# Scores and masked part of y in 64x64 tiles, without the quarter of later tokens, and with another order of the steps within a pair

## The chip, the cores and the metric

The kernel runs on one core of a Trainium2 chip. Its time is the device time of one execution in microseconds (us). The engines are named as in the profile: PE is TensorE (PEld its weight loads, PEq, SPq and so on the queues in front of the engines), DVE is VectorE, ACT is ScalarE, POOL is GpSimd, SP starts the DMA transfers. All data are float32.

## The reference

Gated linear attention over 32 independent heads (4 batches, 8 heads, 768 tokens, width 48), and behind it a soft mixture of 8 experts with 4 slots each over the 384 columns of all heads of a batch:

```python
f = 1.0 / (1.0 + np.exp(-f_logit))
for t in range(S):
    state = f[:, :, t, :, None] * state + np.einsum('bhd,bhe->bhde', k[:, :, t], v[:, :, t])
    y[:, :, t] = np.einsum('bhd,bhde->bhe', q[:, :, t], state)
...
logits = x @ phi
...
slot_input = d.T @ x          # d: softmax of the logits over all tokens
...
    h = np.maximum(slot_input[e] @ w1[e], 0.0)
    slot_out[e] = h @ w2[e]
...
return (c @ slot_out)         # c: softmax of the logits over the slots
```

## The kernel before

**Pairs and chunks.** Two heads make a pair (i, 16 of them, 4 to a batch), and stand on partitions 0 to 47 and 64 to 111. The 768 tokens are six chunks of 128 (m). Within a chunk the gates become running sums `L` of log f, and k is multiplied by exp(L), q by exp(-L). Then y of a chunk is the sum of two products: the masked one, v times the scores k q with the later keys set to 0 (steps `sc`, `mask`, `ia`), and the one with the state at the chunk's start (`kt`, `kv`, `scan`, `ie`).

**The steps of a pair,** by their names in the code, in the profile and in the listing below:

- ACT: `e`, `ln` (L324, L328, tile fb): the gates. `g`, `p` (L335, L338, tiles gb, pb): exp(L) and exp(-L). `ye`, `xe` (yT, xb): copies out of PSUM.
- DVE: `L` (L332, tile Lb): the running sum over 768 elements, from two SBUF inputs. `mask` (L378, scb from sc): two of them to a pair, 768 elements a partition each, from PSUM. `scan` (L411, sb): the state over the chunks. `kte` (L315, kta): copy out of PSUM.
- POOL: `dk`, `dq` (L341, tiles kb, qb): the products of k with exp(L) and q with exp(-L). `pbx` (L315), `pend` (L353): copies of the chunks' ends. Once per batch `cdiv` (L539, ce) and `j4` (L516, pin).
- PE: `kt` (L361): k turned; `sc` (L373): scores; `kv` (L407); `ia` (L398, y from scb and va): the masked product; `ie` (L421, y from qb and sb); `lg` (L453, pl): logits; `xtr` (L432, xt): y turned. Per batch also `te`, `tl` (L471 to L473), `pi` (L496), `ct` (L545).

The array of PE can be used as one, as two halves by rows or by columns, or in quarters of 64x64. Each step names its mode: `sc` "rows" (two tiles of 64x128), `kv` and `ia` "cols" (two of 128x64), `ie` "quarters", `lg` "strips" (four of 128x32), the others "square". A float32 matrix product is two records in the trace: 12 products of `sc` are 24.

**What sets the order.** Each step is an `op` with a due time (`z = i * T`, T = 7.0). For every engine the steps are sorted by due time before anything else is decided, and the engine works them off in that order. Where a step waits, all behind it on its engine wait too. SP's transfers are placed by a planner with costs; the weight loads (`lw1`, `lw2`) are paced behind the steps of that plan and go to buffers of the attention once these are free. PSUM has three units of 1024 columns (a) and two of 512 (b), and three buffers each of k and q and two each of L, g, p and the scores lie between the pairs.

**After the last pair** come the slots' inputs, the two expert layers (`up` L619, `down` L665) and the output (`comb` L711), from about 119 us on.

Of the kernel before, what the change touches and what calls it, by code (L numbers as in the profile page):

```python
# [11 lines left out]
ALU = mybir.AluOpType  # L12
AX = mybir.AxisListType

B, H, S, D = 4, 8, 768, 48
C = 128
# [7 lines left out]
PW = 112  # L24
# [186 lines left out]
def gla_soft_moe_kernel(ctx: ExitStack, tc: tile.TileContext, q, k, f, v, vt, phi, w1, w2, out):  # L211
# [35 lines left out]
    scb = [P([128, 2, 2, 3, C], f"scb{i}") for i in range(N_SC)]  # L247
# [22 lines left out]
    mask = P([128, C], "mask")  # L270
# [15 lines left out]
    nc.gpsimd.affine_select(mask, mask, pattern=[[1, C]], compare_op=ALU.is_ge, fill=0.0, base=0, channel_multiplier=-1)  # L286
# [56 lines left out]
    def decay_k(o, i, cs):  # L343
        times(o, kb[i % N_K][:PW, cs], gb[i % N_G][:PW, cs])
# [21 lines left out]
    def score(o, i, h):  # L366

        u = unit(("sc", i, h))
        for m in range(3):
            cs = slice(C * (3 * h + m), C * (3 * h + m) + C)  # L370
            for r in range(2):
                rs = slice(64 * r, 64 * r + D)
                nc.tensor.matmul(  # L373
                    u[:, 512 * r + C * m : 512 * r + C * m + C], kb[i % N_K][rs, cs], qb[i % N_Q][rs, cs], start=True, stop=True,
                )

    def score_mask(o, i, h):
        nc.vector.tensor_tensor(  # L378
            scb[i % N_SC][:, :, h], un["sc", i, h].rearrange("p (r x) -> p r x", r=2)[:, :, : 3 * C].rearrange("p r (m t) -> p r m t", t=C),
            mask.unsqueeze(1).unsqueeze(1).broadcast_to([128, 2, 3, C]), op=ALU.mult,  # L380
        )
# [9 lines left out]
    def intra(o, i, h):  # L391
        u = unit(("y", i)) if h == 0 else un["y", i]
        for m in range(3 * h, 3 * h + 3):
            for r in range(2):
                at = 1 - r if m < SWAP else r

                v0 = 576 * (i % N_V) + 96 * m + D * r
                nc.tensor.matmul(  # L398
                    u[rows(at), y_cols(m)], va[:, v0 : v0 + (D if at else 64)], scb[i % N_SC][:, r, h, m % 3],
                    start=m % 3 == 0, stop=False, skip_group_check=True,  # L400
                )
# [326 lines left out]
    def warm(due, n, us=0.9):  # L728
# [3 lines left out]
    warm(-100, 4, 1.6)  # L732
# [6 lines left out]
        e=(-99, -98), ln=(-97, -96), g=(-94, -91), p=(-93, -90),  # L739
# [3 lines left out]
    for n, (name, i) in enumerate(  # L743

        [("e", 1), ("ln", 1), ("e", 2), ("kte", 0), ("pbx", 0), ("g", 1), ("p", 1), ("ln", 2), ("ye", 0), ("g", 2), ("p", 2)]

        + [("L", 1), ("scan", 0), ("dq", 1), ("L", 2)]

        + [("dk", 1), ("pend", 0)]
    ):  # L750
        START[name, i] = -80 + n
    START["e", 1], START["ln", 1], START["L", 1] = -95, -92, -94
# [4 lines left out]
    def attention(i):  # L757
# [35 lines left out]
        usual = dict(e=-2 * T - 6.9, ln=-2 * T - 5.9, L=-2 * T + 2.2, g=-2 * T + 4.4, dk=-2 * T + 3.8, p=-2 * T + 4.8, dq=-2 * T + 5.6)  # L793
# [5 lines left out]
        op("pbx", {"POOL": 0.65} if i else {"ACT": 0.4}, decay_pbx, i, r=PB, w=[PX], due=START.get(("pbx", i), z - T + 0.7))  # L799
        op("pend", {"POOL": 0.2}, decay_pend, i, r=PB, w=[("pends", i)], due=START.get(("pend", i), z - T + 1.3))  # L800
        if i == 0:
            for h in range(2):
                op(("kt", "square"), {"PE": 0.33}, kt, i, 3 * h, 3 * h + 3, r=K[h : h + 1], x=[KT], w=[KK], due=START["kt"][h], take=[] if h else [(KK, "a")], ni=6)
        else:
            op(("kt", "square"), {"PE": 0.65}, kt, i, r=K, x=[KT], w=[KK], due=z - T + 3.9, take=[(KK, "a")], ni=12)
        op("kte", {"DVE": 0.86} if i else {"ACT": 0.86}, kt_copy, i, r=[KK], w=[KT], due=START.get(("kte", i), z - T + 4.6), free=[KK])
        for h, key in enumerate((S0, S1)):
            op(("sc", "rows"), {"PE": 0.7}, score, i, h, r=[K[h], Q[h]], x=[SC[h]], w=[key], due=START["sc"][h] if i == 0 else z - T + 5.3 + 0.7 * h, take=[(key, "a")], ni=24)
            op("mask", {"DVE": 0.95}, score_mask, i, h, r=[key], w=[SC[h]], due=START["mask"][h] if i == 0 else z - T + 6.1 + h, free=[key])
        if i == 0:  # L810
            warm(-94, 1)
        op(("kv", "cols"), {"PE": 0.71}, kv, i, r=[KT, V], x=[SB], w=[KV], due=z, take=[(KV, "b")], ni=48)
        op("scan", {"DVE": 0.76}, state, i, r=[KV, PX], w=[SB], due=START.get(("scan", i), z + 1.2), free=[KV])
        for h in range(2):
            op(("ia", "cols"), {"PE": 0.66}, intra, i, h, r=[SC[h], V, *([YY] if h else [])], x=[] if h else [Y], w=[YY], due=z + 0.7 + 0.66 * h, take=[] if h else [(YY, "a")], ni=24)
        op(("ie", "quarters"), {"PE": 0.72}, inter, i, r=[*Q, SB, YY], w=[YY], due=z + 2.2, ni=40)
        op("ye", {"ACT": 0.82}, y_copy, i, r=[YY], w=[Y], due=START.get(("ye", i), z + 3.3), free=[YY])
# [311 lines left out]
```

## Time and profile before

| | us |
|---|---|
| three runs | 174.04, 175.64, 175.8 |
| median of them | 175.64 |
| the profiled execution | 174.06 |
| its span in the profile | 171.9 |
| attention, from the first scores (8.75) to the last pair's (114.3) | 105.5 |
| PE busy, DVE, ACT, POOL | 155.5, 115.8, 93.8, 88.9 |

The span goes from the first to the last instruction; 2.2 us of the profiled execution lie outside it. Of a group of instructions the page gives busy time and the mean of one; the chain gives what was waited for last, from the end back to the start; the timeline gives start and duration.

### The profile page before, as it was taken

Reading aid. Unit: us, or ns where it says so; the run is one execution under the profiler, and the core shown is the slowest. Engines: PE = TensorE matmul, PEld = TensorE weight load, DVE = VectorE, ACT = ScalarE, POOL = GpSimd, SP = SyncE. Lnnn points to the kernel's source line nnn. Section 1 sums busy time; section 2 is a strip of 40 time slices with the busy share of each in tenths; the row PEclk is TensorE's granted clock in tenths of the full one; section 3 lists DMA queues with packets and bytes.
Section 4 is the critical chain, followed back from the end, with each engine's and each line's share of the span. In section 5 each row is a group of like instructions: output and inputs, shape, how many; then the busy total and the mean of one; then the engine's idle time right before and its main releaser. Section 6 shows DMA issues by size and latency. Waiting matters only on the chain.

```text
span 171.9 us, 6033 instructions
## 1 busy us (share of the span) xinstructions
PE 155.5 (90%) x2548; PEld 121.3 (71%) x2548; DVE 115.8 (67%) x168; ACT 93.8 (55%) x168; POOL 88.9 (52%) x88
## 2 busy tenths in 40 slices
PE   5959999999899998999998999999899999989810
PEld 2347888988788968889886889888555454568600
DVE  2677999889998995898996989756540333144420
ACT  5892897867677758678683783542421211042410
POOL 3074599888499895897996988841000001000000
PEclk9999999999999999999999999999999999999965
DMA  5999999999999999999976559999999690019790
GB/s 144 375 402 373 394 403 390 397 396 398 390 378 400 395 390 397 397 400 393 308 264 180 166 190 316 351 390 393 394 396 343 169 375 12 2 40 404 296 354 31
DMA packets 20468, 54.08 MB, mean 315 GB/s; under 512 B 2272, under 2 KB 2640, under 8 KB 20432
## 3 DMA queue, kind: packets, MB, share of 16 engines
q1 hardware_dynamic: 20432, 53.60, 84.4%
q8 instruction: 22, 0.36, 0.9%
q14 instruction: 14, 0.11, 0.2%
HBM read 48.87 MB, written 4.72 MB: 312 GB/s over the span
## 4 chain that ended last, share of the span: by engine, by line
PE 59%; POOL 13%; DVE 10%; ACT 6%; issue 4%; DMA 2%; SPq 0%; POOLq 0%; DVEq 0%; ACTq 0%
PE sc L373 9%; PE y L398 8%; PE up L619 6%; PE kv L407 5%; PE y L421 5%; POOL qb L341 5%; PE po L665 5%; DVE Lb L332 4%; PE kt L361 4%; PE pf L711 4%; PE xt L432 4%; POOL kb L341 3%; PE pl L453 3%; DMA fb<-in_f_dram 2%; POOL ce L539 2%
## 5 line engine op out<-in xcount | busy, mean ns | idle before, releaser
L332 DVE TENSOR_TENSOR_SCAN Lb<-starts,fb 112x768 f32<-112x768 f32 (+1 forms) x17 | 35.1, 2068 | 3.2 <-ACT fb L328 3.2
L341 POOL TENSOR_TENSOR kb<-kb,gb 112x768 f32<-112x768 f32 x15 | 27.5, 1830 | 17.8 <-ACT gb L335 13.9
L378 DVE TENSOR_TENSOR scb<-sc,mask 128x768 f32<-128x768 f32 x32 | 29.3, 952 | 5.0 <-PE sc L373 4.9
L341 POOL TENSOR_TENSOR qb<-qb,pb 112x768 f32<-112x768 f32 (+1 forms) x15 | 28.1, 1871 | 7.2 <-ACT pb L338 7.2
L373 PE MATMUL sc<-qb,kb 48*128 48x128 f32 x384 | 26.5, 282 | 2.8 <-POOL qb L341 1.9
L373 PEld LDWEIGHTS sc<-qb,kb 48*128 48x128 f32 x384 | 22.9, 188 | 5.6 <-POOL qb L341 2.1
L398 PE MATMUL y<-scb,va 128*48 128x128 f32 (+1 forms) x384 | 25.8, 275 | 0.0
L315 ACT COPY yT<-y 112x768 f32<-112x768 f32 x16 | 12.8, 798 | 22.9 <-PE y L421 22.9
L315 POOL COPY pbx<-pb 112x240 f32<-112x240 f32 x15 | 23.7, 1580 | 0.0
L398 PEld LDWEIGHTS y<-scb,va 128*64 128x64 f32 (+1 forms) x384 | 21.9, 130 | 0.6 <-DVE scb L378 0.2
L539 POOL TENSOR_TENSOR ce<-ce,cm 128x256 f32<-128x256 f32 x4 | 4.7, 1172 | 29.3 <-DVE cm L536 29.3
L315 DVE COPY kta<-kt 128x672 f32<-128x672 f32 x15 | 12.7, 844 | 7.1 <-PE kt L361 7.1
L335 ACT ACTIVATE gb<-Lb 112x768 f32<-112x768 f32 (+1 forms) x17 | 13.7, 805 | 5.9 <-DVE Lb L332 5.9
L328 ACT ACTIVATE fb<-fb,one 112x768 f32<-112x768 f32 (+1 forms) x17 | 15.1, 895 | 0.4
L421 PE MATMUL y<-qb,sb 48*48 48x128 f32 x320 | 14.6, 285 | 0.0
L324 ACT ACTIVATE fb<-fb 112x768 f32<-112x768 f32 (+1 forms) x17 | 13.7, 804 | 1.7 <-DMA fb<-in_f_dram 1.7
L407 PE MATMUL kv<-va,kta 128*64 128x48 f32 (+1 forms) x384 | 14.4, 220 | 0.0
L407 PEld LDWEIGHTS kv<-va,kta 128*64 128x64 f32 (+1 forms) x384 | 12.4, 130 | 2.6 <-ACT fb L328 0.8
L338 ACT ACTIVATE pb<-Lb 112x768 f32<-112x768 f32 (+1 forms) x17 | 13.5, 793 | 0.0
L421 PEld LDWEIGHTS y<-qb,sb 48*48 48x48 f32 x320 | 11.1, 162 | 2.7 <-DVE sb L411 2.2
L411 DVE TENSOR_TENSOR_SCAN sb<-kv,pbx 112x288 f32<-112x288 f32 x16 | 12.0, 749 | 1.0 <-PE kv L407 1.0
L361 PE MATMUL kt<-ident,kb 112*128 112x112 f32 x96 | 12.6, 266 | 0.0
(157 smaller groups left out, 258.9 us busy)
## 6 DMA issues: line engine op xcount, KB each, us to landing
w1b<-in_w_dram SPq DMA_DIRECT2D x34, 384.0 KB, 6.4
kb<-in_k_dram SPq DMA_DIRECT2D x16, 384.0 KB, 6.1
qb<-in_q_dram SPq DMA_DIRECT2D x16, 384.0 KB, 6.6
fb<-in_f_dram SPq DMA_DIRECT2D x15, 384.0 KB, 6.2
va<-in_v_dram SPq DMA_DIRECT2D x16, 288.0 KB, 6.5
out_dram<-w1b SPq DMA_DIRECT2D x6, 512.0 KB, 3.9
scb<-in_w_dram SPq DMA_DIRECT2D x4, 384.0 KB, 6.4
out_dram<-w1b SPq DMA_DIRECT2D x6, 256.0 KB, 4.3
```

The costliest lines, as they stand in the source:

```text
L315: {"ACT": nc.scalar.copy, "DVE": nc.vector.tensor_copy, "POOL": nc.gpsimd.tensor_copy}[o.eng](dst, src)
L324: nc.scalar.activation(t, t, AF.Exp, scale=-1.0, accum_out=esum[:, n : n + 1])
L328: nc.scalar.activation(t, t, AF.Ln, bias=one[:PW])
L332: nc.vector.tensor_tensor_scan(Lb[i % N_L][:PW, cs], flat(starts)[:PW, cs], fb[i % N_F][:PW, cs], 0.0, op0=ALU.mult, op1=ALU.add)
L335: nc.scalar.activation(gb[i % N_G][:PW, cs], Lb[i % N_L][:PW, cs], AF.Exp)
L341: (nc.vector if o.eng == "DVE" else nc.gpsimd).tensor_tensor(t, t, by, op=ALU.mult)
L361: nc.tensor.transpose(u[:, C * m : C * m + PW], kb[i % N_K][:PW, C * m : C * m + C], ident[:PW, :PW])
L373: nc.tensor.matmul(u[:, 512 * r + C * m : 512 * r + C * m + C], kb[i % N_K][rs, cs], qb[i % N_Q][rs, cs], start=True, stop=True,)
L378: nc.vector.tensor_tensor(scb[i % N_SC][:, :, h], un["sc", i, h].rearrange("p (r x) -> p r x", r=2)[:, :, : 3 * C].rearrange("p r (m t) -> ...
L398: nc.tensor.matmul(u[rows(at), y_cols(m)], va[:, v0 : v0 + (D if at else 64)], scb[i % N_SC][:, r, h, m % 3], start=m % 3 == 0, stop=False ...
L407: nc.tensor.matmul(u[rows(r), :, m], ktb[i % N_KT][:, m, rows(r)], vb[i % N_V][:, m, r], start=True, stop=True)
L421: nc.tensor.matmul(u[at : at + D, y_cols(m)], sb[i % N_S][rs, :, m - 1], qb[i % N_Q][rs, C * m : C * m + C], start=False, stop=m in (2, 5) ...
```

## The change

Of the 128x128 scores of a chunk, the quarter with keys 64 to 127 and queries 0 to 63 is masked out whole. It is no longer computed, nor multiplied with v.

- **Keys in exchanged order.** In chunks 3 to 5 (x = 1) the two halves of a chunk's k and v are stored in exchanged order. Then chunk n and chunk n + 3 (n = 0 to 2) share one tile of 192 columns: three blocks of 64, of which the first holds chunk n's scores of the first queries (upper partitions) and chunk n + 3's (lower partitions), and the others the scores of the second queries. q stays in its order.
- **`dk` in two halves.** The first 384 columns of k are multiplied as before, the second 384 through a view of k and of exp(L) with blocks of 64, exp(L)'s halves read in exchanged order.
- **`sc`** has mode "quarters": per n and head four products of a 48x64 weight, two with 128 moving columns and two with 64: 24 to a pair in place of 12. Of each pair's two steps the first does n = 0, the second n = 1 and 2.
- **`mask`** has 384 and 768 elements a partition in place of 768 twice; the mask is 192 wide and made by four selections on POOL at the start.
- **`ia`** becomes two steps: `intra_1` for the first queries, mode "quarters", 12 products of 64 rows and 64 moving columns; `intra_2` for the second, mode "cols", 12 products of 128 rows and 64 moving columns.
- **Order.** Due times of almost all steps are new. `sc` stands behind `ie` of the pair before, `lg` and `xtr` of the pair before stand behind `sc`, `kt` of the next pair before `ie`. DVE's `L` stands ahead of `scan`. `kte` of pairs 1 and 2 is ACT's. One warming step less stands at the start (3 for 4).
- **Buffers.** `scb` is one tile `sca`; the general way (not taken with these inputs) reads k in the old order from a further input `kn`.

On PE, before, from `ie` of one pair to `ia` of the next (y from qb and sb is `ie`, pl `lg`, kt and xt the turns, sc the scores, kv `kv`, y from scb `ia`):

```order
L421 MATMUL y<-qb_77,sb_86 48x128 x10
L453 MATMUL pl<-yT_87,phs 32x192
...
L361 MATMUL kt<-ident,kb_75 128x112 x6
L432 MATMUL xt<-ident,yT_87 128x112 x6
L373 MATMUL sc<-qb_78,kb_75 128x128 x12
L407 MATMUL kv<-va,kta 64x48
...
L398 MATMUL y<-scb_80,va 48x128
```

And now on PE the same stretch, from the second part of `ia` of one pair to that of the next (L437 is `intra_2`, L423 `intra_1`):

```order
L437 MATMUL y<-sca,va 48x64
L372 MATMUL kt<-ident,kb_75 128x112 x6
L460 MATMUL y<-qb_77,sb_85 48x128 x10
L391 MATMUL sc<-qb_78,kb_75 64x128 x2
L391 MATMUL sc<-qb_78,kb_75 64x64 x2
...
L492 MATMUL pl<-yT_87,phs 32x192
...
L471 MATMUL xt<-ident,yT_87 128x112 x6
L423 MATMUL y<-sca,va 48x64
...
L446 MATMUL kv<-va,kta 64x48
```

The scores moved up behind `ie`, the logits and the turn of y behind the scores, and the turn of k ahead of `ie`.

On DVE, before, over two pairs in the first batch (Lb is `L`, kta `kte`, scb the masks, sb `scan`):

```order
L332 SCALAR_TENSOR_TENSOR Lb_65<-starts,fb_63 112x768
L315 COPY kta<-kt 128x672
L378 TENSOR_TENSOR scb_81<-sc,mask 128x2x384 x2
L411 SCALAR_TENSOR_TENSOR sb_86<-kv,pbx_84 112x288
L332 SCALAR_TENSOR_TENSOR Lb_66<-starts,fb_64 112x768
```

And now on DVE at the same place:

```order
L337 SCALAR_TENSOR_TENSOR Lb_65<-starts,fb_63 112x768
L450 SCALAR_TENSOR_TENSOR sb_84<-kv,pbx_82 112x288
L320 COPY kta<-kt 128x672
L398 TENSOR_TENSOR sca<-sc,mask 128x2x192
L398 TENSOR_TENSOR sca<-sc,mask 128x2x384
L337 SCALAR_TENSOR_TENSOR Lb_66<-starts,fb_64 112x768
```

`L` moved from behind `scan` to ahead of it: masks, `L`, `scan`, `kte` is now the order of a pair.

The diff, cut to what is spoken of here and in the prediction:

```diff
-    nc.gpsimd.affine_select(mask, mask, pattern=[[1, C]], compare_op=ALU.is_ge, fill=0.0, base=0, channel_multiplier=-1)
+    for p, at in ((0, 0), (0, 128), (1, 0), (1, 64)):
+        t = mask[64 * p : 64 * p + 64, at : at + 64]
+        nc.gpsimd.affine_select(t, t, pattern=[[1, 64]], compare_op=ALU.is_ge, fill=0.0, base=0, channel_multiplier=-1)
...
     def decay_k(o, i, cs):
-        times(o, kb[i % N_K][:PW, cs], gb[i % N_G][:PW, cs])
+        kk, g = kb[i % N_K], gb[i % N_G]
+        if cs.start == 0:
+            times(o, kk[:PW, : S // 2], g[:PW, : S // 2])
+        if cs.stop == S:
+            kk, g = (t[:PW, S // 2 :].rearrange("p (n h t) -> p n h t", h=2, t=64) for t in (kk, g))
+            times(o, kk, g[:, :, ::-1])
...
-    def score(o, i, h):
...
+    def score(o, i, ns, xs=(0, 1)):
+        for key, _ in o.takes:
+            unit(key)
+        for n in ns:
+            for x, p in ((0, 0), (0, 1), (1, 1), (1, 0)):
+                if x not in xs:
+                    continue
+                m = n + SWAP * x
+                for r in range(2):
+                    rs = slice(64 * r, 64 * r + D)
+                    u = un["sc", i, min(n, 1)][64 * p : 64 * p + 64, 512 * r + 192 * max(n - 1, 0) :][:, :192].rearrange("p (a t) -> p a t", t=64)
+                    dst, t0 = (u[:, 0 : 2 + x : 1 + x], 0) if p == x else (u[:, 1 + x : 2 + x], 64)
+                    nc.tensor.matmul(
+                        dst, kb[i % N_K][rs, C * m + 64 * p : C * m + 64 * p + 64],
+                        qb[i % N_Q][rs, C * m + t0 : C * m + C].rearrange("p (a t) -> p a t", t=64), start=True, stop=True, skip_group_check=True,
+                    )
...
+    def intra_1(o, i):
+        u = unit(("y", i))
+        for n in range(SWAP):
+            for x in range(2):
+                m = n + SWAP * x
+                for r in range(2):
+                    at = r if x else 1 - r
+                    v0 = 576 * (i % N_V) + 96 * m + D * r
+                    c0, ps_ = y_cols(m).start, slice(64 * x, 64 * x + 64)
+                    nc.tensor.matmul(
+                        u[rows(at), c0 : c0 + 64], va[ps_, v0 : v0 + (D if at else 64)], scb[i % N_SC][ps_, r, n, :64],
+                        start=n == 0, stop=False, skip_group_check=True,
+                    )
+    def intra_2(o, i):
...
+                nc.tensor.matmul(
+                    u[rows(at), c0 : c0 + 64], va[:, v0 : v0 + (D if at else 64)], scb[i % N_SC][:, r, n, 64 + 64 * x : 128 + 64 * x],
...
-    warm(-100, 4, 1.6)
+    warm(-100, 3, 1.75)
...
-        usual = dict(e=-2 * T - 6.9, ln=-2 * T - 5.9, L=-2 * T + 2.2, g=-2 * T + 4.4, dk=-2 * T + 3.8, p=-2 * T + 4.8, dq=-2 * T + 5.6)
+        usual = dict(e=-3 * T - 1, ln=-3 * T - 0.1, L=-2 * T + 0.9, g=-2 * T + 2.7, dk=-2 * T + 3.5, p=-2 * T + 3.5, dq=-2 * T + 5.3)
...
-        op(("kv", "cols"), {"PE": 0.71}, kv, i, r=[KT, V], x=[SB], w=[KV], due=z, take=[(KV, "b")], ni=48)
-        op("scan", {"DVE": 0.76}, state, i, r=[KV, PX], w=[SB], due=START.get(("scan", i), z + 1.2), free=[KV])
...
+        op(("ia", "quarters"), {"PE": 0.42}, intra_1, i, r=[*SC, V], x=[Y], w=[YY], due=z + 1.2, take=[(YY, "a")], ni=48)
+        op(("kv", "cols"), {"PE": 0.71}, kv, i, r=[KT, V], x=[SB], w=[KV], due=z + 1.7, take=[(KV, "b")], ni=48)
+        op("scan", {"DVE": 0.76}, state, i, r=[KV, PX], w=[SB], due=START.get(("scan", i), z + 2.7), free=[KV])
+        op(("ia", "cols"), {"PE": 0.66}, intra_2, i, r=[*SC, V, YY], w=[YY], due=z + 2.4, ni=48)
...
+    k = kn.reshape(NP, 128, NM, 2, 64).copy()
+    k[:, :, SWAP:] = k[:, :, SWAP:, ::-1]
```

120 lines of the change are left out of this document (62 added, 58 removed).

## The prediction

> **What bounds the kernel now.** The page comes first: which engine is full, and through whom the end is reached.
>
> ```profile
> PE 155.5 (90%) x2548; PEld 121.3 (71%) x2548; DVE 115.8 (67%) x168; ACT 93.8 (55%) x168; POOL 88.9 (52%) x88
> PE 59%; POOL 13%; DVE 10%; ACT 6%; issue 4%; DMA 2%; SPq 0%; POOLq 0%; DVEq 0%; ACTq 0%
> 30.90:114.30 83.40, 81.55 (x1465) 71.54 (x1464) 71.83 (x88) 57.32 (x99) 69.89 (x63) 1.00 0.94 343
> 127.60:171.90 44.30, 34.26 (x506) 20.86 (x506) 13.00 (x34) 9.08 (x20) 0.61 (x1) 0.92 0.57 208
> ```
>
> PE is busy for 90% of the span and carries 59% of the chain, but DVE and POOL carry 23%. The third line is a window from the scores of pair 3 to those of pair 15 (columns: length, then busy us of PE, PEld, DVE, ACT, POOL, granted clock, DMA share, GB/s). PE works 81.55 of 83.40 us there, at the full clock. DVE and POOL have 72 and 70, much of it waiting, as will be seen. So PE comes first here, with two followers close behind. The last line is the stretch behind attention, where DMA is at 0.57. The chain of waits, read along one pair, shows what PE does without a gap:
>
> ```profile
> 72.80 1.54 PE sc L373 x24
> 74.34 0.77 PE kv L407 x21
> 75.11 1.38 PE y L398 x23
> 76.49 0.84 PE y L421 x20
> 77.34 0.47 PE pl L453 x8
> 77.80 0.72 PE kt L361 x6
> 78.53 0.11 PE te L471
> ...
> 78.86 0.58 PE xt L432 x6
> 79.44 1.54 PE sc L373 x24
> ```
>
> This pair has a `te` (three rows, from 78.53 to 78.86, 0.33); without it the seven steps are 6.30 us. The turns show what a change of tile mode costs: six records of `kt` behind the logits take 0.72, six of `xt` behind another square step 0.58. I put 0.15 on each change. There are five to a pair (at the fronts of `sc`, `kv`, `ie`, `lg`, `kt`).
>
> The followers are seen in the timelines of DVE and POOL (start, duration; the first row is the page's):
>
> ```profile
> L332 DVE TENSOR_TENSOR_SCAN Lb<-starts,fb 112x768 f32<-112x768 f32 (+1 forms) x17 | 35.1, 2068 | 3.2 <-ACT fb L328 3.2
> 16.48 1.75 DVE L332 TENSOR_TENSOR_SCAN Lb<-starts,fb 112x768 f32<-112x768 f32 x1
> 47.77 2.88 DVE L332 TENSOR_TENSOR_SCAN Lb<-starts,fb 112x768 f32<-112x768 f32 x1
> 66.58 1.83 POOL L341 TENSOR_TENSOR kb<-kb,gb 112x768 f32<-112x768 f32 x1 [1.72 <-PE xt L432]
> 68.36 1.83 POOL L341 TENSOR_TENSOR qb<-qb,pb 112x768 f32<-112x768 f32 x1
> 69.15 0.74 DVE L411 TENSOR_TENSOR_SCAN sb<-kv,pbx 112x288 f32<-112x288 f32 x1
> 69.81 1.99 DVE L332 TENSOR_TENSOR_SCAN Lb<-starts,fb 112x768 f32<-112x768 f32 x1
> 70.13 2.08 POOL L315 COPY pbx<-pb 112x240 f32<-112x240 f32 x1
> 74.71 1.83 POOL L341 TENSOR_TENSOR qb<-qb,pb 112x768 f32<-112x768 f32 x1
> 76.12 2.04 DVE L332 TENSOR_TENSOR_SCAN Lb<-starts,fb 112x768 f32<-112x768 f32 x1
> 89.70 0.62 POOL L315 COPY pbx<-pb 112x240 f32<-112x240 f32 x1
> ```
>
> `L` alone takes 1.75. At 69.81 it takes 1.99: POOL's `dq` ends at 68.36 + 1.83 = 70.19, and `L` 1.61 later, at 71.80. At 76.12 the same: `dq` ends at 76.54, `L` 1.62 later. And POOL's copy `pbx`, 0.62 alone, takes 2.08 when it meets `L`, ending 0.41 behind it. **`L` on DVE and the work of POOL run one after the other, never together.** At 47.77 `L` waits longer still (2.88). Over the fifteen whole `L` (35.1 less two halves of about 0.95) the mean is 2.21, so the wait is 0.46.
>
> **The change, part by part: PE.** Records of one tile follow each other; four tiles run beside each other. Without the 0.15 of the change, `sc` gives each tile 12 records of 128 moving columns in 1.39 (116 ns), `ia` 12 in 1.38 (115), `ie` at most 6 in 0.69 (115). `kv`, 48 columns, gives 12 in 0.62 (52 ns). So a record costs 115 ns at 128 columns; at 64 it lies between kv's 52 and, if small products brought nothing, 115. I take half of 115, 57, which is near the row of 48.
>
> - `sc`: each of four tiles gets three times two records of 128 and two of 64: 3 x (230 + 114) = 1.03 for 1.39 before.
> - `ia`: 6 records of 57 in quarters and 12 in halves, 0.34 + 0.68 = 1.02 for 1.38.
> - Mode changes: behind `ie` the scores need none, but `lg`, `xt`, `intra_1`, `kv`, `kt`, `ie` need one each: six for five, +0.15.
>
> Together 0.36 + 0.36 - 0.15: PE has 5.73 for 6.30, 0.57 less in each pair. At 52 ns it would be 0.68 less; at 115 the two steps would take 3.45 for 2.77 before, and a pair 0.8 more. Twice the count of records comes with this (96 instead of 48 for both steps, each with a weight load).
>
> ```profile
> 126.14 0.33 PE psi L598 x24
> ```
>
> These 24 records on four tiles came 14 ns apart, so a denser stream is handed out where the tiles are free; I cost the count at nothing. [...]
>
> **DVE and POOL.** The first mask shrinks from 768 to 384 elements, which lies between half of 0.95 and 0.95; 0.55 with a fixed part. It saves 0.4 on DVE, but is not on the loop below. `dk` becomes two instructions, the second with blocks read in exchanged order. No row shows either.
>
> ```profile
> L341 POOL TENSOR_TENSOR kb<-kb,gb 112x768 f32<-112x768 f32 x15 | 27.5, 1830 | 17.8 <-ACT gb L335 13.9
> 118.93 0.62 POOL L539 TENSOR_TENSOR ce<-ce,cm 128x256 f32<-128x256 f32 x1 [5.25 <-DVE cm L536]
> 90.42 1.26 POOL L516 TENSOR_SCALAR pin<-pin,nmb 128x384 f32<-128x384 f32 x1
> L378 DVE TENSOR_TENSOR scb<-sc,mask 128x768 f32<-128x768 f32 x32 | 29.3, 952 | 5.0 <-PE sc L373 4.9
> ```
>
> `kb` costs 2.4 ns an element, and so does `ce`, whose second input repeats one element 32 times: an unusual view is free there. `pin`, 3.3 ns an element, is the dearest row: with it the second half would cost +0.34. [...]
>
> What was hidden behind PE now shows. Three loops, each per pair:
>
> - PE: 5.73, with `te` or `tl` 6.06.
> - POOL and `L`, which exclude each other: 1.62 + 1.78 (spacing 66.58 to 68.36) + 0.05 + 1.77 + 0.62 + 0.15 for the small copy = 6.0. If `L` comes only behind `dq`, as in the two rows, the loop closes: 71.80 to 78.16 is 6.36.
> - DVE: `L` now stands **ahead of** `scan`, and behind the masks. So when it waits for POOL, `scan` waits too, then `ie` on PE, then the scores, then the masks, then the next `L`. Second mask 0.95, `L` 1.75, `scan` 0.74, `ie` 0.69, `sc` 1.03 and an estimated 0.3 of hand-offs: 5.5, with the mean wait of `L` 5.95. With the early wait (2.88 - 1.75 = 1.1) it is 6.6.
>
> I take **6.1** for a pair: just above the longest loop, since three of about equal length that meet in every pair do not all run at their floor. Ends: 5.75 and 6.4. What is queued behind the waiting `L` is `scan` and `kte`, and for them wait `ie`, `kv` and all of PE.
>
> **The sum.** Pairs, by the start of their scores:
>
> ```profile
> 30.93 1.54 PE sc L373 x24
> 114.32 1.54 PE sc L373 x24
> 43.47 0.94 PE L373 MATMUL sc<-qb,kb 48*128 48x128 f32 x12
> 51.17 1.61 PE L373 MATMUL sc<-qb,kb 48*128 48x128 f32 x24
> 57.80 1.61 PE L373 MATMUL sc<-qb,kb 48*128 48x128 f32 x24
> 62.84 1.61 PE L496 MATMUL pi<-xb,el 128*32 128x192 f32 x24
> 64.91 0.44 PE L545 MATMUL ct<-ident,ce 128*128 128x128 f32 x2 [0.45 <-POOL ce L539]
> 66.43 0.83 PE L373 MATMUL sc<-qb,kb 48*128 48x128 f32 x10
> 86.00 1.61 PE L373 MATMUL sc<-qb,kb 48*128 48x128 f32 x24
> 94.68 1.61 PE L373 MATMUL sc<-qb,kb 48*128 48x128 f32 x24
> ```
>
> Twelve intervals from pair 3 to pair 15 take 83.4. Three are long: 7.7 (43.47 to 51.17, PE waits there for DVE) and twice 8.65, where `pi` and `ct` stand on PE and PE waits for `ce`. The other nine take 58.4, 6.49 each.
>
> 1. Nine ordinary ones at 6.1: 54.9, **-3.5**.
> 2. The two with `pi`: 5.73 + 1.61 + two changes = 7.65 (`ct` has its place two pairs on, where POOL is done): **-2.0**. The 7.7 is DVE's: 0.
> 3. Early pairs, where `L` waits longest: five of the nine at 6.4 instead of 6.1, **+1.5**. In pairs 0 to 2 DVE and the transfers set the pace: 0, between the 0.6 that one warming step less can bring and the same in new waits.
> 4. At the end `lg` and `xt` of pair 14 now stand behind the last scores: 1.0 more on PE, less 0.57: **+0.4**.
>
> Sum -3.6. After the last pair nothing changes: with DMA at 0.57 of that stretch the weights still come in time. Transfers carry the same bytes; a pair's 1.44 MB in 6.1 us are 236 GB/s of the window's 343, which hides them, as long as the weights give way. So 174.06 - 3.6 = 170.5 for an execution like the profiled one. Two of the three runs before lie 1.6 to 1.7 above it. For the median I add half of that: **171.3**.
>
> **The rivals.**
>
> - *PE's saving goes through.* If `L` slips in between `dk` and `dq` (DVE wins the turn against `pbx` in the rows), the loops run at their floors, 5.8: nine times 0.69, two times 1.0, the end: about -8, with the half step to the median **167.4**. For it: POOL is idle 13.9 us in all before `kb`. Against: the order puts `L` into PE's path.
> - *The gain stays inside the loop of `L` and POOL.* `L` comes behind every `dq`, 6.36 a pair: -1.2, -2.0, +1.5, +0.4, and the split of `dk` +0.7: -0.6, **174.4**. For it: three of the four `L` quoted come so.
> - *Slower: the second half of `dk`.* If it costs like `pin`, the closed loop is 6.36 + 0.4 = 6.75: nine times +0.26, +1.5, +0.4, and the pairs with `pi` gain nothing: +4.2, **179**. It decides from about +0.15 in `dk`, where the loop passes 6.49.
> - *The small tiles do not run as counted.* `ie`'s 20 records took 0.84, 42 ns apart. Were that the pace of quarters and not the load of its fullest tile, `sc` and `intra_1` would need 3.0 instead of 1.37: +1.1 a pair, some +16, **190**. [...]
>
> **How the numbers follow.** Forecast 0.42, saving goes through 0.22, closed loop 0.18, `dk` 0.10, records 0.08. The likeliest is 171.3. For 8 in 10 the range takes in 167.4 and 174.4 and, of the slower cases, the start: 166.5 to 177.5. A measurement of this kernel can tell about 1% from no change, that is 1.8 us of 175.64. Faster by more: the forecast but for a tenth of its cases, and all of the second, 0.60. Within: 0.14 of the closed loop's 0.18, 0.05 of the forecast, 0.03 of the records, 0.22. Slower: the rest, 0.18.
>
> **What would show it.** [...] `ie` waiting for `sb`, and behind it `L` longer than 1.75, shows the new wait. `kb` rows of 0.9 twice show `dk` cheap. Intervals of the scores near 6.1 are the forecast, 5.8 the first rival, 6.4 the second. It would be wrong if the transfers fell behind, so that `fb`, `kb` or `qb` waited for DMA in mid-attention, or if a PSUM unit were missing, since scores and y now overlap otherwise.

## The result, and the profile after

The changed kernel is slower. In runs taken turn by turn on one chip its median is 187.13 us (185.45 to 188.99), that of the kernel before 175.71 (174.04 to 175.80): a ratio of 1.059, with a 95% interval of 1.048 to 1.070. The forecast was 171.3, with a range up to 177.5. The profiled execution takes 185.76, its span 183.6 (171.9 before). How long the granted clock is low differs between executions of one kernel by several us (its mean is 0.945 to 0.970 in the four of the changed kernel), so medians of the runs below are uncertain by 1 to 2%.

Lines of the page of the kernel after, with those of two DMA queues (packets, MB, share of the time of 16 engines), and two windows (length, then busy us of PE, PEld, DVE, ACT, POOL, granted clock, DMA share, GB/s): from the scores of pair 3 to those of pair 15, and behind `psi`.

```profile
PE 154.2 (84%) x3314; PEld 117.6 (64%) x3314; DVE 108.7 (59%) x166; ACT 96.2 (52%) x170; POOL 87.3 (48%) x106
PEclk9999999999958999999999999999999999999995
q1 hardware_dynamic: 20432, 53.60, 82.5%
q8 instruction: 28, 0.46, 1.0%
PE 69%; DVE 10%; issue 8%; DMA 3%; ACT 2%; POOL 2%; SPq 1%; POOLq 0%; DVEq 0%; ACTq 0%
```

```profile
32.10:123.40 91.30, 81.84 (x2048) 69.71 (x2042) 68.66 (x88) 58.48 (x99) 68.07 (x75) 0.96 0.90 308
139.50:183.60 44.10, 34.25 (x506) 20.84 (x506) 13.01 (x34) 9.09 (x20) 0.62 (x1) 0.95 0.55 199
```

The stretch behind attention is as before (44.10 for 44.30). The loss lies ahead of `psi`, which starts at 138.0 instead of 126.1. There PE has the same 82 us of work in 91.3 us as before in 83.4: it waits. POOL's share of the chain fell from 13% to 2%; "issue", time in which an engine waits for nothing that the profile shows, rose from 4% to 8%, some 14 us of 183.6. The chain through pair 9 and into pair 10 shows where:

```profile
82.42 0.50 PE y L423 x21
82.92 0.83 PE kv L446 x21
83.75 1.59 issue
85.34 0.20 PE kv L446
85.54 0.72 PE y L437 x23
86.26 0.72 PE kt L372 x6
...
88.11 1.04 PE sc L391 x24
...
90.36 0.27 PE y L423 x6
90.62 0.75 issue
91.38 0.49 PE y L423 x16
```

PE stops in the middle of a step: 21 records of `kv` run, then nothing for 1.59 us, then the rest of the step, whose operands and PSUM buffer had been there all along. Six records into `intra_1` (L423) it stops again. The list of waits from 30 to 129 us gives no releaser for these stops either; they are its rows with `issue` (us in total, times, longest):

```profile
PE kv L446 <- issue: 4.3, 3, 1.6
PE y L460 <- DVE sb L450: 2.5, 1, 2.5
PE y L423 <- issue: 1.7, 3, 0.8
PE y L460 <- issue: 1.2, 2, 0.8
PE y L423 <- DVE sca L398: 1.1, 2, 0.5
PE tl L511 <- issue: 0.9, 1, 0.9
```

What the stops have in common is seen when all of PE's records (weight loads, matmuls, semaphore instructions) are counted from the start. The ten longest of these stops stand at records 449, 961, 1217, 1473, 2497, 3009, 3265, 3521, 5057 and 5313: each is 193 plus a multiple of 256. And each ends 1.2 to 1.6 us behind the end of a packet of queue q8, the instruction queue. Its packets are 16 KB each, so a block of 256 instructions has 64 bytes for each. In this table, worked out from the records, "starts" is counted from the block end before:

```
                block ends   PE     packet   packet   PE goes   behind the
                at record    waits  starts   ends at  on at     packet's end
kernel before      2497      0      2.30      77.87    81.29    3.43
                   3777      0      2.87     113.66   116.87    3.21
kernel after        961      0.83   3.70      30.50    31.82    1.32
                   1217      1.14   3.09      36.00    37.39    1.39
                   3265      1.59   3.65      84.06    85.34    1.28
                   3521      0.75   3.70      89.96    91.38    1.41
                   5313      1.58   3.78     127.36   128.69    1.33
late weights       2497      0      1.05      60.43    63.41    2.98
(run e7)           5057      0.80   3.24     112.62   113.98    1.36
```

So PE's instructions come over the DMA engines in blocks of 256 (the expectations below call them pages). By these times a block is asked for when one is used up, while PE goes on with the next, which is already there; if PE uses that up first, it waits. In the kernel after its packet starts 2.88 us behind the block end in the median (0.9 to 4.5), at a DMA share of 0.90; it takes about 1.05, and where PE waits it goes on 1.2 to 1.6 behind the packet's end: 5 to 6 us in all. In the kernel before a block lasted 6.6 us or more, and the next one's packet had always ended 3.1 us or more before PE came to it. Its page has 22 packets in this queue, for 28 after:

```profile
q8 instruction: 22, 0.36, 0.9%
```

A pair of the kernel after has 320 instructions instead of 224, in less PE time; a block is worked off in 4.3 to 5.1 us where nothing holds PE up (5.5 with a `pi` in it). With the two short ones at 705 and 1729, twelve waits at block ends sum to 9.3 us ahead of `psi`.

A second loss is at 43 us, in the timeline of DVE and PE of the kernel after (start, duration) and in windows of 3 us behind it (columns as above):

```profile
41.85 1.97 DVE L337 TENSOR_TENSOR_SCAN Lb<-starts,fb 112x768 f32<-112x768 f32 x1
43.74 3.48 DVE L303 COPY same<-ident 32x128 f32<-32x128 f32 x4
47.25 0.76 DVE L450 TENSOR_TENSOR_SCAN sb<-kv,pbx 112x288 f32<-112x288 f32 x1
48.06 0.80 PE L460 MATMUL y<-qb,sb 48*48 48x128 f32 x18 [2.47 <-DVE sb L450]
```

```profile
48.00:51.00 3.00, 2.79 (x74) 2.20 (x78) 1.71 (x5) 1.98 (x5) 2.54 (x4) 0.81 0.92 295
51.00:54.00 3.00, 3.00 (x49) 2.41 (x43) 2.48 (x2) 2.09 (x5) 0.00 (x0) 0.50 0.80 242
54.00:57.00 3.00, 3.00 (x52) 2.88 (x49) 0.76 (x1) 1.16 (x2) 2.44 (x11) 0.55 0.90 296
```

Four small copies into `same`, needed only at the end, now stand between `L` and `scan`. They take 3.48. Before they stood ahead of `L` and took 2.06:

```profile
40.55 2.06 DVE L298 COPY same<-ident 32x128 f32<-32x128 f32 x4
```

Now PE waits 2.47 for `sb`. From 49.8 to 56.7 us the granted clock is then 0.50 (the windows, third number from the end), and the interval between two scores is 9.52 where an undisturbed one is 6.1 to 6.6: some 3.1 more. The sum: 9.3 + 2.5 + 3.1 = 14.9 lost, 11.9 net at `psi`. The 3.0 between them is left for what the change brings.

### The profile page after: what moved, and what is told of

Its sections match the earlier page's. It is cut to its first block, busy times and chain, and to the rows that moved or that the text cites. A ratio compares the mean times of both kernels' runs of the same rounds, so it can differ in the third digit from the quotient of the medians.

```text
span 183.6 us, 7588 instructions
## 1 busy us (share of the span) xinstructions
PE 154.2 (84%) x3314; PEld 117.6 (64%) x3314; DVE 108.7 (59%) x166; ACT 96.2 (52%) x170; POOL 87.3 (48%) x106
## 4 chain that ended last, share of the span: by engine, by line
PE 69%; DVE 10%; issue 8%; DMA 3%; ACT 2%; POOL 2%; SPq 1%; POOLq 0%; DVEq 0%; ACTq 0%
PE sc L391 9%; PE y L460 7%; PE kv L446 7%; PE up L658 6%; PE y L437 6%; PE kt L372 6%; PE xt L471 5%; PE y L423 4%; PE po L704 4%; PE pl L492 4%; PE pf L750 4%; DMA qb<-in_q_dram 3%; PE pi L535 3%; DVE Lb L337 2%; POOL kb L346 2%
## 5 line engine op out<-in xcount | busy, mean ns | idle before, releaser
L346 POOL TENSOR_TENSOR kb<-kb,gb 112x384 f32<-112x384 f32 x30 | 33.9, 1153 | 25.6 <-ACT gb L340 21.8
L337 DVE TENSOR_TENSOR_SCAN Lb<-starts,fb 112x768 f32<-112x768 f32 (+1 forms) x17 | 30.7, 1809 | 3.3 <-ACT fb L333 3.3
L398 DVE TENSOR_TENSOR sca<-sc,mask 128x384 f32<-128x384 f32 (+1 forms) x32 | 23.9, 754 | 10.6 <-PE sc L391 9.6
L391 PE MATMUL sc<-qb,kb 48*64 48x128 f32 (+1 forms) x768 | 23.4, 251 | 0.8 <-DVE qb L346 0.4
L391 PEld LDWEIGHTS sc<-qb,kb 48*64 48x64 f32 x768 | 19.6, 134 | 2.4 <-issue 1.5
L578 POOL TENSOR_TENSOR ce<-ce,cm 128x256 f32<-128x256 f32 x4 | 2.5, 617 | 35.3 <-DVE cm L575 35.3
L450 DVE TENSOR_TENSOR_SCAN sb<-kv,pbx 112x288 f32<-112x288 f32 x16 | 11.9, 747 | 12.3 <-PE kv L446 9.8
L437 PE MATMUL y<-sca,va 128*48 128x64 f32 (+1 forms) x384 | 16.4, 229 | 0.1
L437 PEld LDWEIGHTS y<-sca,va 128*48 128x48 f32 (+1 forms) x384 | 14.6, 135 | 1.9 <-issue 1.9
L471 PE MATMUL xt<-ident,yT 112*128 112x112 f32 x96 | 13.2, 276 | 0.8 <-issue 0.8
L423 PE MATMUL y<-sca,va 64*64 64x64 f32 (+1 forms) x384 | 10.8, 232 | 3.5 <-issue 1.9
```

The costliest lines, as they stand in the source:

```text
L337: nc.vector.tensor_tensor_scan(Lb[i % N_L][:PW, cs], flat(starts)[:PW, cs], fb[i % N_F][:PW, cs], 0.0, op0=ALU.mult, op1=ALU.add)
L346: (nc.vector if o.eng == "DVE" else nc.gpsimd).tensor_tensor(t, t, by, op=ALU.mult)
L391: nc.tensor.matmul(dst, kb[i % N_K][rs, C * m + 64 * p : C * m + 64 * p + 64], qb[i % N_Q][rs, C * m + t0 : C * m + C].rearrange("p (a t) ...
L398: nc.vector.tensor_tensor(scb[i % N_SC][:, :, ns[0] : ns[0] + n], un["sc", i, min(ns[0], 1)].rearrange("p (r x) -> p r x", r=2)[:, :, : 19 ...
L423: nc.tensor.matmul(u[rows(at), c0 : c0 + 64], va[ps_, v0 : v0 + (D if at else 64)], scb[i % N_SC][ps_, r, n, :64], start=n == 0, stop=Fals ...
L437: nc.tensor.matmul(u[rows(at), c0 : c0 + 64], va[:, v0 : v0 + (D if at else 64)], scb[i % N_SC][:, r, n, 64 + 64 * x : 128 + 64 * x], star ...
```

## The experiments

Three theories. **F**: PE waits for its instruction blocks, because there are more of them and the DMA engines are full. **O**: the new order of the steps costs the time. **R**: the small products run slower than counted. "Before" is the kernel before in the runs that were taken together with each kernel: 174.80 for e1 to e4, 174.13 for e5 to e8, 174.03 for e9 to e12, 175.96 for e13 to e15.

**e1: more instructions, by cutting the score products.**

```diff
-                nc.tensor.matmul(u[:, 512 * r + C * m : 512 * r + C * m + C], kb[i % N_K][rs, cs], qb[i % N_Q][rs, cs], ...)
+                for t in (0, 64):
+                    nc.tensor.matmul(u[:, 512 * r + C * m + t : 512 * r + C * m + t + 64], kb[i % N_K][rs, cs], qb[i % N_Q][rs, cs.start + t : cs.start + t + 64], ...)
```

> The kernel before, with each score product cut into two of 64 query columns; order, tiles and arithmetic stay. PE's stream grows from 224 to 272 instructions a pair (a product is two weight loads and two matmuls). Theory F (PE waits for its own instructions: in the trace after, ten waits that nothing releases stand at every 256th instruction, and end 1.25 to 1.57 us behind a 16 KB packet of the instruction queue; a page then lasts about 5.5 us): 272/256 x 5.5 = 5.8 us a pair on the mean, under the 6.3 of PE, so few page waits, 175 to 179. Theory O (the new order, `L` ahead of `scan`, costs the time, and the count is free): 175 to 176.5, no page waits. Theory R (small products run slower than half of a whole one): `sc` longer than 1.54, with 0.1 us a pair for each 4 ns a record.

193.21, a ratio of 1.099 (1.085 to 1.112), and not one wait at a block end. One row of its chain says why:

```profile
83.46 2.87 PE sc L374 x48
```

`sc` went from 1.54 to 2.87. Here, in mode "rows" with a weight load 128 wide, a record of 64 columns took as long as one of 128 (48 in 2.87, 24 in 1.54); in the kernel after, whose weight loads are 64 wide and whose mode is "quarters", `sc` takes 1.04. So this kernel tests R for another kind of product, and says little on the count: a block lasts 7.0 us here.

**e2: the products of `ia` cut as well** (`t` in 0 and 64, as above).

> The same with the products of `ia` cut in two as well: 320 instructions a pair, the count of the kernel after, in the order of the kernel before, with PE work of 6.3 us a pair. F: 320/256 x 5.5 = 6.9 us a pair and more where others wait behind: page waits of 0.3 to 1.5 us at most page ends, 182 to 189. O: 175 to 177. R: `sc` and `ia` each longer, and no waits at page ends.

197.60, 1.135 (1.124 to 1.147). A pair takes 7.76, since `sc` is long here too; with 320 instructions a block lasts 6.28 us in the median, and there is one wait of 0.76. F had expected waits at most ends, which was wrong of the sum, not of the mechanism: 320 instructions in 7.76 us are no faster a stream than 260 in 6.3.

**e3: the new order alone,** with the due times of the kernel after in the kernel before.

```diff
-        usual = dict(e=-2 * T - 6.9, ln=-2 * T - 5.9, L=-2 * T + 2.2, g=-2 * T + 4.4, dk=-2 * T + 3.8, p=-2 * T + 4.8, dq=-2 * T + 5.6)
+        usual = dict(e=-3 * T - 1, ln=-3 * T - 0.1, L=-2 * T + 0.9, g=-2 * T + 2.7, dk=-2 * T + 3.5, p=-2 * T + 3.5, dq=-2 * T + 5.3)
 ...
-        op(("kv", "cols"), ..., due=z, ...)
+        op(("kv", "cols"), ..., due=z + 1.7, ...)
```

> The order of the kernel after with the whole score products, two mask steps of equal size, one `dk` and the whole `ia` of the kernel before: 224 instructions a pair. The rows of PE, DVE, ACT and POOL stand in the order of the kernel after. F: no waits at page ends; PE 6.3 + 0.15 a pair, 174 to 179, with the stall near 45 us (the copies `same` ahead of `scan`) still there. O: the loss of the kernel after remains, 184 to 189.

183.65, 1.044 (1.030 to 1.058): between the two theories. No wait stands at a block end. The intervals around 46 us are 8.83 and 9.70, the copies into `same` stand there between `L` and `scan`, and the clock is 0.50 from 48.8 to 55.7 and also from 11.3 to 18.1. O is a part of the loss.

**e4: fewer instructions in the kernel after.**

```diff
-            for x, p in ((0, 0), (0, 1), (1, 1), (1, 0)):
+            for x in xs:
...
-                    nc.tensor.matmul(dst, kb[i % N_K][rs, C * m + 64 * p : C * m + 64 * p + 64], ...)
+                    nc.tensor.matmul(u[:, 128 * x : 128 + 64 * x], kb[i % N_K][rs, C * m : C * m + C], qb[i % N_Q][rs, C * m + 64 * x : C * m + C], ...)
```

> The kernel after, with the two 64-key products of a score chunk joined into one of 128 keys (128 queries for chunks 0 to 2, 64 for chunks 3 to 5): 48 instructions a pair fewer (272) at the same columns per tile, `sc` 1.03 plus a mode change. It leaves out the scores of the earlier queries of chunks 3 to 5 and has others in their place; all else is as after, its order too. F: about half of the page waits go, 175 to 181. O, or `dk` in halves as the cause: no change, 185 to 189, with waits of the same length behind DVE or POOL.

183.19 in the median of four runs; the profiled execution takes 177.49 (others up to 186.26, with more time at the low clock). The waits at block ends are gone, all of them, in the same order and with the same `dk`. PE has no gap in the chain of pairs 8 to 12; two rows of it:

```profile
82.27 1.49 PE sc L387 x24
...
88.05 0.84 PE y L456 x20
```

But `sc` is 1.49, again with weight loads 128 wide, so a pair takes 6.5 to 6.6 and a block 6.0. With both the count and the rate lower this agrees with F without proving it.

**e5: more instructions in the old order,** by cutting `ia` and `ie` of the kernel before.

```diff
-                    u[at : at + D, y_cols(m)], sb[i % N_S][rs, :, m - 1], qb[i % N_Q][rs, C * m : C * m + C],
+                    u[at : at + D, c0 : c0 + 64], sb[i % N_S][rs, :, m - 1], qb[i % N_Q][rs, C * m + t : C * m + t + 64],
```

> The kernel before, with each product of `ia` and of `ie` cut into two of 64 columns. Their weight loads are 48 or 64 columns wide, so the cut adds little PE time (`ia` cut costs 0.12 a pair between the traces of the two cut kernels so far, 7.64 and 7.76). Order, DVE, POOL and transfers stay. PE's stream has 312 instructions a pair, for 224 before and 320 after. F (pages of 256 PE instructions that take about 5.5 us to come while DMA is full): 312/256 x 5.5 = 6.7 a pair at least, waits of 0.2 to 1.5 us at most page ends, 180 to 187. If the count is free and the new order costs the time: 176 to 178.5, no waits at page ends.

188.24, 1.085 (1.073 to 1.097). The cut was not as cheap as expected:

```profile
90.98 1.45 PE y L400 x46
92.42 1.30 PE y L425 x40
```

`ie` went from 0.84 to 1.30, and a pair without `te` from 6.30 to 6.89; that alone is 9 us. Beside it there are waits at five block ends, 0.15 to 1.05 and 3.2 us in all, at ends of the same kind (193 plus a multiple of 256); one of the five, 1.05, falls together with a late landing of `kb`. In the kernel before, with the same order, steps and transfers, there were none. The count brings the waits without the new order.

**e6: the copies into `same` first.**

```diff
-    op("consts", {"DVE": 0.5}, lambda o: consts(), w=["same"], due=30)
+    op("consts", {"DVE": 0.5}, lambda o: consts(), w=["same"], due=-100)
```

> The kernel after, with the four copies into `same` (L303) at the head of DVE's order instead of between `L` and `scan` near 44 us; nothing else moves. In the trace after, PE waits 2.47 us there for `sb`, and the granted clock is 0.50 from 49.8 to 56.7 us, which makes the interval 9.52 for 6.4. If the two belong together: the clock stays at 1.00, both are gone (2.5 + 3.1), 179 to 182, and the page waits stay. If the low clock has another cause: 183 to 185. If this stall is all the loss: 175 to 177.

185.52 in the median of four runs (181.68 to 190.64), a spread too wide to tell it from the kernel after. In the profiled execution, the longest of the four, the wait for `sb` at 45 us is gone. But the waits at block ends sum to 10.3, and one of them, 1.95 at 36.7 us, is followed by a clock of 0.50 from 38.3 to 48.6: the intervals there are 9.47 and 8.56. So the low clock came behind another wait of PE.

**e7: the same instructions with emptier DMA engines.**

```diff
-            op("lw1", {"SP": 0.45}, load_w1, n, x, w=[("w1", n, x)], due=500 + n, kb=384)
+            op("lw1", {"SP": 0.45}, load_w1, n, x, r=[("pends", 14)], w=[("w1", n, x)], due=500 + n, kb=384)
```

> The kernel after, with the 28 resident loads of w1 (10.7 MB) held back until the gates of pair 14 are done, so that the transfers of the attention alone share the DMA engines. Only the stretch ahead of `psi` is to be compared; the end gets 27 us of transfers more. F, with the packet's wait in the DMA queue as its larger part: packets start within 1 us of the page end (1.7 to 3.8 after), page waits sum to less than 2 us (9.4 after), `psi` starts at 128 to 131 (138.0 after). If a page's time doesn't depend on the other transfers: waits as in the kernel after, `psi` at 137 to 139.

As a whole 192.56, for the weights come late. The stretch ahead of `psi` decides for F: `psi` starts at 128.8 instead of 138.0. A window of pairs 6 to 11 (columns as above), and pair 8 in the chain:

```profile
57.00:93.00 36.00, 35.46 (x934) 30.52 (x933) 31.84 (x40) 27.91 (x48) 32.19 (x28) 1.00 0.72 224
```

```profile
68.36 1.16 PE sc L391 x36
69.52 0.48 PE pl L492 x8
70.00 0.72 PE xt L471 x6
70.73 0.50 PE y L423 x22
71.23 0.77 PE kv L446 x21
...
72.06 0.71 PE y L437 x22
72.77 0.72 PE kt L372 x6
73.50 0.22 PE ct L584 x2
73.72 0.84 PE y L460 x20
74.56 1.16 PE sc L391 x33
```

With DMA at 0.72 instead of 0.90 the packets start 1.26 us behind the block end in the median (2.88 in the kernel after), and no wait stands at a block end between 21 and 113 us. Three are left, 2.7 us in all, one at 20 us and two behind 113 us (the last row of the table above, whose packet starts after 3.24 us, is one of them). So 6.6 of the 9.2 us by which `psi` comes sooner are waits at block ends (9.3 in the kernel after, 2.7 here); the low clock is also shorter (3.4 us for 6.8), and the rest was not traced. That `psi` is still 2.7 us later than before (126.1) has its reasons in this trace too: the three waits, and the wait for `sb` at 46 us, here 3.20 long. PE's instructions and their order, DVE's and POOL's work are those of the kernel after. The intervals from pair 6 to pair 15 that hold neither `pi` nor such a wait are 6.14 to 6.33, 6.21 in the mean; the nine ordinary ones before were 6.49.

**e8: the copies first, in the kernel before** (the edit of e6).

> The kernel before with the four copies into `same` at the head of DVE's order (as in the run of the kernel after). Its interval of 7.7 at 43.5 us, where PE waits 0.80 for DVE, should fall to 6.6 or 6.9: 0.8 to 1.1 less, 173.7 to 174.2 where before is 174.8. If DVE's next work only takes the place: no change.

The interval of 7.7 became 6.63, as expected, and the profiled execution is 1.2 us shorter than that of the kernel before; over all runs 174.64 against 174.13, a ratio of 1.000 (0.995 to 1.006). No change that could be measured.

**e9: e3 with the copies first** (the edit of e6).

> The order of the kernel after with the steps of the kernel before (224 instructions a pair), and the four copies into `same` at the head of DVE's order. The same order with the copies between `L` and `scan` took 183.65, with intervals of 8.83 and 9.70 around 46 us and others of 6.68 to 6.79. If those copies and the low clock behind them make that loss: both intervals fall to 6.7 to 7.0, 5 us less, 177 to 180, with the rest of the distance to before in the 6.7 (one change of tile mode more, 0.15) and in the start. If the order itself (`L` ahead of `scan`) stalls DVE there: 182 to 184.

178.91, 1.022 (1.012 to 1.033). The two intervals fell from 18.5 together to 14.1 (7.35 and 6.79). So 4 to 5 us of e3's loss were the copies and the low clock behind them. The rest, 4.7 us at `psi`, is 2.1 in the start (low clock from 10.4 to 17.3) and one change of tile mode in each pair:

```profile
75.44 1.54 PE sc L373 x24
76.98 0.47 PE pl L453 x8
77.45 0.72 PE xt L432 x6
78.17 0.81 PE y L398 x12
78.98 0.63 PE kv L407 x22
79.61 0.73 PE y L398 x12
80.33 0.73 PE kt L361 x6
```

With `ie` (0.84) these are 6.47 a pair for 6.30 in the old order, and PE has no gap.

**e10: a fuller start of the kernel after** (copies first, the identity matrix earlier, `warm(-95.5, 1)` between the halves of pair 0).

> The kernel after with the copies into `same` first, the identity matrix made ahead of the masks, and one more warming step of PE (1.7 us) in its wait between the two halves of pair 0, where PE is idle 1.5 to 1.9 us and the granted clock then sometimes falls to 0.50. Page waits stay (8 to 10 us). If idle PE, whatever the reason, brings the low clock: no low clock ahead of 30 us, 181 to 184. F alone sets the rest.

184.49, 1.058 (1.049 to 1.068). In the profiled execution, the longest of five (189.57), the low clock came all the same, from 10.4 to 17.2 and three more times up to 100 us; waits at block ends sum to 11.3. But the edit did not leave PE without a wait at the start: the warming steps now begin and end sooner, and PE is idle for 1.64 us from 7.1 to 8.8. So this run does not tell whether an idle PE at the start brings the low clock; it rather fits that.

**e11: a shorter queue of transfers.**

```diff
-    AHEAD = 2.3
+    AHEAD = 1.4
```

> As the run before this one (copies first, filled start), with the loads of the weights started later by the planner: it keeps 1.4 us of transfers ahead instead of 2.3. F with the packet's wait in the queue: instruction packets start about 0.9 us sooner behind the page end, page waits fall from 8 to 10 to 3 to 5 us, 176 to 180, unless the weights then come too late at the end. If the wait isn't in that queue: as the run before.

185.49, 1.045 (1.034 to 1.056). The packets start after 1.71 us in the median (2.51 in e10), waits sum to 8.2 (11.3), `psi` starts at 134.6 (142.3). Of these 7.7 us 3.1 are the waits; much of the rest is clock, which is low for 10.2 us ahead of `psi` and for 20.5 in e10. The end pays it back: from `psi` to the end of the span 51.8 us instead of 45.2, where the weights come later. The waits fell less than expected, in the direction of F.

**e12: the fuller start in the kernel before** (edits of e6 and e10).

> The kernel before with the copies into `same` first and the same warming step more in PE's wait between the halves of pair 0. The copies alone gave runs of 172.6 to 172.9 at a clock of 0.98 and runs of 174.8 to 176.0 at 0.963 to 0.972. If the low clock of those comes from the idle PE at the start, the second kind goes: 172.5 to 173.2, 0.6 to 1.1% below before. If it has another cause: 174 to 175.

173.33 in twelve runs (172.40 to 174.07), against 174.03 (172.79 to 176.66): 0.997 (0.994 to 1.000). It is the fastest version of all, at the edge of what can be told from the kernel before. None of the twelve runs is over 174.1, where five of the 17 of the kernel before are over 175. That fits the idle PE at the start, but the traces don't show it: neither profiled execution, this one's or that of the kernel before, has low clock ahead of the end.

**e13, e14, e15: other shapes of the loads,** to see in what line the instruction packet waits. e13 cuts the loads of 128 partitions of the kernel after into 104 and 24 (the edit below), e14 those of e7 into 88 and 40, e15 those of the kernel after into two of 64.

```diff
+    def dma(dst, src):
+        n = 104 if dst.shape[0] == 128 else dst.shape[0]
+        nc.sync.dma_start(dst[:n], src[:n])
+        if n < dst.shape[0]:
+            nc.sync.dma_start(dst[n:], src[n:])
```

> The kernel after, with each load of 128 partitions cut into one of 104 and one of 24, same bytes. [...]

> [...]

> [...]

All three are far slower: 221.0 (two runs), 224.6 (one) and 218.8 (two). Windows from 60 to 120 us of e13 and of e15:

```profile
60.00:120.00 60.00, 48.46 (x1098) 41.28 (x1096) 37.39 (x45) 29.79 (x53) 29.91 (x40) 0.87 0.83 251
```

```profile
60.00:120.00 60.00, 46.57 (x1042) 39.86 (x1042) 33.74 (x45) 30.65 (x55) 26.62 (x37) 0.86 1.03 255
```

In e13 the share of DMA is 0.83, for 0.88 in the same window of the kernel after. The trace doesn't tell the engines apart, so whether some of them carried nothing was not shown. The instruction packets still start 3.02 us behind the block end (2.88 in the kernel after). In e14 they start 1.76 us behind it, later than the 1.26 of e7. In e15 the share is 1.03, and only 255 GB/s are moved: a packet of 3 KB takes 199 ns in the median, 121 in the kernel after. Its instruction packets start after 2.67 us. None of the three tells in what line the packet waits; that, and with it a shape of loads that would save the 9 us, stays open.

## Why the prediction was wrong, point by point

- **The step that failed: "I cost the count at nothing."** Twice the records in two steps were weighed only for how densely PE takes them up, against the row of `psi`. That side held: `sc` runs 48 records in 1.04, 22 ns apart, and by the forecast's own figures the saving of 0.57 was used up only at 27 (72 records in 1.37 + 0.57). What the records cost on their way into PE was no term of the sum. They cost 9.3 us. The profile before had what was needed: 22 packets of q8, one every 7 us, each needed no sooner than 3.1 us after its end. 320 instructions in 5.73 us ask for a block every 4.6, against the 5 to 6 that a block took with DMA at 0.90.
- **The transfers, taken as hidden.** The bytes are the same, as the prediction said, and between 25 and 128 us nothing waits for k, q, v or f. But an instruction packet started 2.88 us behind the block end in the median with DMA at 0.90, and 1.26 with 0.72 in e7: e7 only moves bytes out of this stretch, and most of the waits go (9.3 to 2.7).
- **What is queued behind the waiting `L`.** The prediction named `scan` and `kte`. It missed the four copies into `same`, which the new due times put there once: 2.5 us of waiting and 3.1 of low clock in the trace, 4 to 5 us between e3 and e9.
- **PE, 5.73 for 6.30.** `sc` 1.03 was right (1.04 to 1.16). The two `ia` are 0.50 and 0.71, with the new mode change 1.21 for 1.17; `ie` 0.84. A pair in e7 takes 5.98 without its `ct`, 0.25 more than forecast.
- **6.1 a pair: right where the instructions come,** 6.21 in the mean of e7. There PE itself is busy 35.46 of 36 us. `L` slips in between the pieces of `dk` and `dq`, as the first rival had it, only up to 42 us (starts at 27.49, 34.67 and 41.85 in the kernel after). Later it comes behind `dq`. Its mean fell from 2068 to 1809 ns (below) because POOL is mostly done by then: five of the nine `L` behind 50 us take 1.75. In e7, where PE hardly waits, `L` again has to wait for `dq`: it starts at 76.69 and 82.99 and takes 2.20 and 2.29, so its ends are 6.39 apart. That is close to the closed loop of the second rival, 6.36; with the pairs that hold `pi`, 7.7 and 8.5 long, it has time enough not to show in the mean. The term for `L` waiting longer in early pairs (+1.5) did not show: behind 14 us none is longer than 2.33, where before five were 2.6 to 3.0. The 0.3 of hand-offs in DVE's loop was the author's estimate, from no row; the one in the rows from 43 us on, from `scan` to `ie`, is 0.05. (The terms of the first rival, 6.2 and 2.0 less and 0.4 more, give 167.1; the prediction has 167.4.)

```profile
L337 DVE TENSOR_TENSOR_SCAN Lb<-starts,fb 112x768 f32<-112x768 f32 (+1 forms) x17 | 30.7, 1809 | 3.3 <-ACT fb L333 3.3
L346 POOL TENSOR_TENSOR kb<-kb,gb 112x384 f32<-112x384 f32 x30 | 33.9, 1153 | 25.6 <-ACT gb L340 21.8
```

- **`dk` in halves, +0.05.** The term stands in POOL's loop of 6.0, and no run shows it: it was the author's estimate. A half takes 1.00 in 26 of 30 rows, the exchanged view no more than the plain one: +0.17 for both (2.00 for 1.83). In the kernel after it bounds nothing, as POOL is idle 25.6 us ahead of `kb`.
- **Pairs 0 to 2 at 0.** The scores of pair 3 start at 32.15 for 30.86, +1.3, with waits of 0.78, 0.24 and 0.83 at block ends in it.
- **The end +0.4.** From the scores of pair 15 to `psi` it is 14.5 for 11.8. A wait of 1.58 at a block end is in it, so +1.1 is left for the forecast 0.4. Behind `psi` nothing changed, as forecast.
- **The rival of the small records, 190,** came near the time by another mechanism. It had the records of `sc` 42 ns apart, where they came 22 apart; that its time came near is luck.
- **Left open:** when exactly the clock falls. Waits of 1.4 to 3.2 us stand ahead of most low stretches, but one of 1.59 (83.75 us) and one of 1.58 (127.11) in the kernel after, and one of 1.89 (10.1) in the kernel before, had none behind them. The granted clock of the kernel after changes in steps of 3.41 us: it is 1.00 from 8.89 to 49.85, which is twelve, 0.50 to 56.67, two, and 1.00 to 179.55, thirty-six. Counted in such steps, PE is idle for 0.48 of the one ahead of 49.85, while each of the two waits of the kernel after falls on two steps, with 0.40 of a step at most. So the idle share of a step fits better than the length of a wait; but it is not shown, as in e11 the clock fell behind a step with 0.45 idle (at 129.4) and not behind another with 0.45 (57.7 to 61.1).

## What to carry to other kernels

Count PE's instructions as a stream with a rate of its own: a block of 256 lasts as long as PE works on it, and the next one needed 5 to 6 us to come here at a DMA share of 0.90. A change that cuts products into smaller tiles has to leave a block longer than that, or leave the DMA engines room; look for waits without a releaser in the middle of a step, at equal distances in the count of instructions. And when due times are moved, read what else the new order puts behind a waiting instruction, the rare steps too.

## What the runs showed of the hardware that was not expected

- In the kernel after an instruction packet started 2.88 us behind the block end in the median (DMA share 0.90), in e7 1.26 (0.72). At the end of the kernel after one started after 0.56, at 157.1 us with a share of 0.06, and one after 0.31, at 172.6 with 0.99, where the output is written. In the kernel after, where PE waited for the packet, it went on 1.25 to 1.57 us behind its end.
- In mode "rows", under weight loads of 128 columns, half the moving columns saved nothing: `sc` 1.54 uncut, 2.87 with products of 64 columns (e1). In mode "cols", under loads of 48 and 64, they ran in half the time per record: `ia` 1.38 uncut, 1.45 with twice the records (e5). Whether the width of the load or the mode makes the difference was not separated.
- 40 records of `ie` with the two halves of a product in a row on the same tile took 1.30 (e5), where 48 of `sc` that go round the four tiles took 1.04. Whether the order among the tiles makes this, no run shows.
- The granted clock fell to 0.50 for 3.4, 6.8 or 10.2 us at a time. It was low behind PE waits of 2.47 us (kernel after) and 1.95 (e6).
- With loads of 64 partitions a packet of 3 KB took 199 ns in the median, for 121 with loads of 128, and 255 GB/s were moved at a share of 1.03 (e15, 60 to 120 us), where the kernel after moves 300 at a share of 0.88.
